# Two key copies from VectorE to ScalarE, and three issue costs in the list scheduler of an attention and feed-forward kernel

## The chip, the cores and the metric

The kernel runs on one core of one Trainium2 chip. The metric is the device time of one execution in microseconds (us), measured on that core. A kernel is executed six times where it is timed, in rounds that alternate with executions of the kernel before on the same chip. A "fast" run is one within 1.5% of the fastest of its kernel.

## The reference, cut to what matters

Attention with a threshold over 8 batches, 8 heads, 576 positions and 64 columns; then a row norm and a gated feed-forward layer over 4608 rows of 512.

```python
scores = (q @ k.transpose(0, 1, 3, 2)) / 8                    # 8 x 8 x 576 x 576
thresh = scores.max(-1, keepdims=True) - tau                  # tau = 0.02
scores = np.where(scores >= thresh, scores, -1e9)
attn = exp(scores - max); attn = attn / (attn.sum(-1) + 1e-9)
x = (attn @ v), heads laid side by side                       # 4608 x 512
xn = x / sqrt(mean(x * x) + 1e-6) * rms_g
out = (silu(xn @ w_gate) * (xn @ w_val)) @ w_out              # 512 -> 1536 -> 512
```

## The kernel before

The program is first written down as a list of operations, each with its engine, an assumed cost in ns, a priority, and the operations it needs. A list scheduler then fixes the order in which each engine's queue is filled. The costs in `COST` do nothing else: they are beliefs, and the chip never sees them.

```python
COST = dict(
    # ... cut: some 30 costs of PE, DVE, ACT and POOL operations ...
    sp=480.0, sp_v=650.0, sp_w=600.0, sp_tr=1300.0, sp_qk=900.0, sp_tl=630.0,     # DMA issues on SyncE
)
# ... cut ...
    seq = order_ops(ops, {"R": 4})        # always takes the operation that it believes can start first
    for o in seq:
        o.fn(o)                           # each call appends to its engine's queue, in this order
```

The work goes in 144 score steps, each a block of 128 query rows by a pair of heads. A step is: scores into PSUM (TensorE, L566); a row reduction per head (VectorE, L589), which also copies the scores out; the threshold from the row maxima (GpSimd, L596); masking and exponential (ScalarE L607 and L614, or with the mask on GpSimd, L626, L640 and L645); a transpose of the weights (on TensorE in early steps, L659, later by DMA); attention times values (L693, L697); the division (VectorE, L714 and L715). When a block has all its heads, its row norm (ScalarE L726, then GpSimd L729, L731, L734) and the feed-forward matmuls (gate L792, value L797, output L853) are dealt between later steps.

```python
    tn = add("POOL", COST["pool_tiny"], s - 4, [ttr_of[s, 0], ttr_of[s, 1]], nthr)     # threshold, L596
    # ...
    pls.append(add("ACT", COST["prelu"], s + 0.5, [tn], prelu))                        # masking pass, L607
    # ... in the row norm of a block:
    bb = add("POOL", COST["pool_mean"], s, [a, o_c], mean)                             # L729, L731
    c = add("POOL", COST["xn"], s - 1, [bb], norm)                                     # L734
```

At the start the keys of the four pairs of heads are transposed on TensorE (L364) and copied out of PSUM in halves, one half by each of two engines (L374):

```python
        def transposed(load, srcs, dsts, prio, engines):
            # ... transposes into one PSUM bank ...
            for e, (eng, lo, hi) in enumerate(engines):
                def ev(o, eng=eng, lo=lo, hi=hi):
                    copy = nc.scalar.copy if eng == "ACT" else nc.vector.tensor_copy
                    # ... copies parts lo to hi ...
        # ... in emit_k, for pair p:
            t, k_ready[p] = transposed(load, [pair(nat[:, 1, c]) for c in range(4)],
                                       [(0, 2, qkT[0][p][:, 1, 0:2]), (2, 2, qkT[0][p][:, 1, 2:4])], prio,
                                       [("DVE", 0, 2), ("ACT", 2, 4)])
```

## Time and profile before

| | kernel before |
|---|---|
| time, median of 3 runs ahead of the change | 567.91 us (567.86 to 568.21) |
| profiled span | 568.3 us |
| TensorE / ScalarE / VectorE / GpSimd busy | 98% / 80% / 75% / 57% |
| my estimate of pure TensorE work | 533 us |

The profiled span belongs to one execution, which took 570.23 us, slower than all six timed executions of the first comparison. So the span is good for finding where time goes, and the timed runs alone say how much it is. The busy table, the chain and the stages are read in the prediction. One more stretch turns out to matter. This is the timeline of the kernel before at 67 us, each line with its start, its duration, engine, line and operation, and in brackets the idle time ahead of it and what ended it:

```profile
67.32 1.28 POOL L645 TENSOR_TENSOR wsb<-wsb,esb 128x576 f16<-128x576 f16 x1
...
69.64 0.69 POOL L734 TENSOR_SCALAR xn<-xsb,ir 128x512 f16<-128x512 f32 x1
...
70.41 0.52 POOL L596 TENSOR_SCALAR nth<-mx 128x2 f32<-128x2 f32 x2
...
70.67 0.77 ACT L607 ACTIVATE ssb<-ssb,nth 128x576 f32<-128x576 f32 x1 [1.92 <-POOL nth L596]
```

GpSimd does a mask (L645), then the whole norm of a block (three instructions, of which the last is shown), and only then the thresholds of steps 19 and 20, the first a job of a quarter of a microsecond for which ScalarE has been idle for 1.92 us.

### The profile page before, as it was taken

What the parts mean: (1) busy time and instruction counts of PE and PEld (TensorE: products, weight loads), DVE (VectorE), ACT (ScalarE), POOL (GpSimd) and SP (SyncE); (2) the same over time, 40 slices, a digit from 0 to 9 for tenths busy, and PEclk for the clock granted to TensorE, in tenths of its full rate; (3) what the DMA queues carried; (4) which work ended last, traced back from release to release, by engine and by line L of the source; (5) the groups of instructions that cost most, each with busy time, mean ns of one, the idle gap of its engine ahead of it and who ended that gap; (6) DMA issues with size and microseconds to landing.
All of it is one profiled execution on the core that took longest, in us unless ns stands there. A gap on an engine that the chain in (4) does not pass through costs nothing.

```text
span 568.3 us, 13686 instructions
## 1 busy us (share of the span) xinstructions
PE 558.4 (98%) x5000; PEld 334.7 (59%) x5000; DVE 427.2 (75%) x1093; ACT 457.4 (80%) x739; POOL 322.4 (57%) x462
## 2 busy tenths in 40 slices
PE   8999999999999999999999999999999999999997
PEld 4666766767676555555555555545555455454674
DVE  4899977969958588758895789659875886586354
ACT  4999899999878787979898898778978897884332
POOL 2378946976747457666766658555666555551000
PEclk9999999999999999999999999999999999999999
DMA  8999998769994686999876799789887565633211
GB/s 187 250 289 282 178 195 184 161 132 202 167 202 104 136 159 149 177 177 187 178 160 148 142 186 181 161 168 162 174 167 184 88 96 86 178 81 44 84 37 38
DMA packets 270019, 88.98 MB, mean 157 GB/s; under 512 B 252544, under 2 KB 262272, under 8 KB 269952
## 3 DMA queue, kind: packets, MB, share of 16 engines
q1 hardware_dynamic: 267168, 86.02, 74.1%
q0 software_dynamic: 1600, 1.57, 1.8%
q8 instruction: 39, 0.64, 0.5%
q10 hardware_dynamic: 1184, 0.52, 0.3%
q14 instruction: 28, 0.23, 0.1%
HBM read 37.75 MB, written 9.44 MB: 83 GB/s over the span
## 4 chain that ended last, share of the span: by engine, by line
PE 89%; DVE 3%; DMA 2%; issue 2%; ACT 2%; POOL 1%; SPq 0%; DVEq 0%; POOLq 0%; ACTq 0%
PE s_ps L566 28%; PE ring L792 16%; PE ring L797 16%; PE ring L853 14%; PE ring L697 6%; PE ring L303 2%; PE ring L693 2%; DVE ssb L589 2%; DMA qkn<-in_q_dram 1%; PE s_ps L831 1%; PE s_ps L853 1%; PE ring L659 1%; PE s_ps L797 1%; PE ring L364 1%; DMA stage<-in_q_dram 1%
## 5 line engine op out<-in xcount | busy, mean ns | idle before, releaser
L589 DVE CUSTOM_DVE_ANT_0 ssb<-s_ps,zrow 128x576 f32<-128x576 f32 x288 | 207.8, 754 | 67.7 <-PE s_ps L566 60.5
L607 ACT ACTIVATE ssb<-ssb,nth 128x576 f32<-128x576 f32 x224 | 165.9, 766 | 32.4 <-POOL nth L596 32.1
L566 PE MATMUL s_ps<-qkt 64*128 64x288 f32 x1024 | 170.2, 429 | 1.4 <-DVE mx L589 1.1
L566 PEld LDWEIGHTS s_ps<-qkt 64*128 64x128 f32 x1024 | 96.2, 186 | 53.5 <-DVE mx L589 16.2
L640 POOL TENSOR_SCALAR wsb<-ssb,nth 128x576 f16<-128x576 f32 x64 | 110.5, 1726 | 9.7 <-DMA wt<-wsb 2.9
L792 PE MATMUL ring<-xnT,wg 128*128 128x512 f16 (+1 forms) x548 | 112.9, 328 | 0.4 <-DVE sl L809 0.4
L797 PE MATMUL ring<-xnT,wv 128*128 128x256 f16 (+1 forms) x544 | 111.4, 327 | 0.6 <-ACT qTv L472 0.3
L596 POOL TENSOR_SCALAR nth<-mx 128x2 f32<-128x2 f32 x144 | 31.6, 220 | 133.9 <-DVE mx L589 120.6
L809 DVE SCALAR_TENSOR_TENSOR sl<-th,ring 128x512 f32<-128x512 f32 (+1 forms) x137 | 75.9, 554 | 25.9 <-ACT th L806 24.6
L614 ACT ACTIVATE wsb<-ssb 128x1152 f16<-128x1152 f32 x80 | 92.9, 1161 | 1.9
L806 ACT ACTIVATE th<-ring 128x512 f32<-128x512 f32 (+1 forms) x137 | 66.3, 486 | 28.9 <-PE ring L792 26.4
L853 PE MATMUL ring<-wo,hf 128*128 128x512 f16 x384 | 89.3, 380 | 0.0
L645 POOL TENSOR_TENSOR wsb<-wsb,esb 128x576 f16<-128x576 f16 x64 | 81.8, 1278 | 8.8 <-ACT esb L626 4.4
L814 DVE TENSOR_TENSOR hf<-ring,sl 128x256 f16<-128x256 f32 (+1 forms) x136 | 75.9, 558 | 10.0 <-PE s_ps L566 0.5
L797 PEld LDWEIGHTS <-wv 128*128 128x128 f16 x576 | 52.2, 98 | 42.9 <-issue 12.3
L792 PEld LDWEIGHTS <-wg 128*128 128x128 f16 x576 | 52.0, 98 | 41.0 <-issue 11.6
L853 PEld LDWEIGHTS <-hf 128*128 128x128 f16 x408 | 37.4, 98 | 47.2 <-issue 6.6
L626 ACT ACTIVATE esb<-ssb,nth 128x576 f16<-128x576 f32 x64 | 49.2, 768 | 7.1 <-POOL nth L596 7.0
L697 PE MATMUL ring<-va,wt 128*128 128x65 f16 (+1 forms) x1264 | 52.8, 193 | 0.0
L697 PEld LDWEIGHTS <-wt 128*128 128x128 f16 (+1 forms) x1280 | 48.7, 100 | 3.4
L611 ACT ACTIVATE wsb<-ssb 128x576 f16<-128x576 f32 x64 | 43.6, 681 | 1.6
L693 PE MATMUL ring<-va,wt 128*128 128x130 f16 (+1 forms) x158 | 35.1, 227 | 0.1
(68 smaller groups left out, 448.1 us busy)
## 6 DMA issues: line engine op xcount, KB each, us to landing
vst<-in_v_dram SPq DMA_DIRECT2D x32, 256.0 KB, 3.2
qkn<-in_k_dram SPq DMA_DIRECT2D x31, 256.0 KB, 3.8
out_dram<-osb SPq DMA_DIRECT2D x31, 256.0 KB, 2.6
qkn<-in_q_dram SPq DMA_DIRECT2D x28, 256.0 KB, 4.1
stage<-in_moe_w_gate_dram SPq DMA_DIRECT2D x6, 512.0 KB, 6.6
stage<-in_moe_w_val_dram SPq DMA_DIRECT2D x6, 512.0 KB, 6.3
wt<-wsb SPq DMA_TRANSPOSE x128, 3.1
wo<-in_moe_w_out_dram POOLq DMA_DIRECT2D x4, 384.0 KB, 7.6
```

The source lines that it names most:

```text
L566: nc.tensor.matmul(s_ps[h][rows, ROW_AT + n * part:ROW_AT + n * part + n], lhs(hs), kT[i][p][h][hs, n * part:n * part + n], start=True, st ...
L589: nc.vector.tensor_tensor_reduce(out=ssb[a][:, h], in0=s_ps[h][:, ROW_AT:ROW_AT + S], in1=zrow, scale=-1.0 / 8.0, scalar=3.0e38, op0=ALU.a ...
L607: nc.scalar.activation(out=ssb[a][:, h], in_=ssb[a][:, h], func=PRELU, scale=-1.0, bias=nth[m][:, h:h + 1], **PRELU_KW)
L614: nc.scalar.activation(out=wsb[s % NW], in_=ssb[a], func=AF.Exp)
L640: nc.gpsimd.tensor_scalar(out=wsb[s % NW][:, h], in0=ssb[a][:, h], scalar1=nth[m][:, h:h + 1], scalar2=None, op0=ALU.is_le)
L645: nc.gpsimd.tensor_tensor(out=wsb[s % NW][:, h], in0=wsb[s % NW][:, h], in1=esb[es], op=ALU.mult)
L697: nc.tensor.matmul(ring[o.slot[0]][rs, at:at + D + 1], w[:, 5 * h + j, rs], va[vi][:, p, 2 * j + h], start=False, stop=(h == 1 and j == 3))
L792: nc.tensor.matmul(ring[o.slot[0]][:, 0:n], wg[d][:, fs], xnT[slot][:, d, 0:n], start=(d == 0), stop=(d == 3))
L797: nc.tensor.matmul(ring[o.slot[0]][:, 0:n], wv[d][:, fs], xnT[slot][:, d, 0:n], start=(d == 0), stop=(d == 3))
L809: nc.vector.scalar_tensor_tensor(out=sl[i][:, 0:n], in0=th[i][:, 0:n], scalar=1.0, in1=ring[g.slot[0]][:, 0:n], op0=ALU.add, op1=ALU.mult)
L814: nc.vector.tensor_tensor(out=hf[hi][:, 0:n], in0=ring[vv.slot[0]][:, 0:n], in1=sl[i][:, 0:n], op=ALU.mult)
L853: nc.tensor.matmul(ring[(first or o).slot[0]], hf[hs[fc][0]][:, 128 * j:128 * (j + 1)], wo[:, fc], start=(fc == 0), stop=(fc == NFC - 1))
```

## The change

The intent: take two copies off VectorE while it is the engine that holds up the first steps, and give the scheduler issue costs on SyncE nearer to those that the trace shows (a key or query load of one issue takes 0.61 to 0.65 us there from 21 to 52 us, but for one of 2.72; the constant was 0.90). No instruction is added or removed.

```diff
-    sp=480.0, sp_v=650.0, sp_w=600.0, sp_tr=1300.0, sp_qk=900.0, sp_tl=630.0,
+    sp=420.0, sp_v=600.0, sp_w=600.0, sp_tr=1300.0, sp_qk=680.0, sp_tl=630.0,
@@
-                                       [("DVE", 0, 2), ("ACT", 2, 4)])
+                                       [("ACT" if p in (1, 2) else "DVE", 0, 2), ("ACT", 2, 4)])
```

## The prediction

> **What bounds the kernel now.** I read the busy table first, then the chain of waits, then busy time by stage, then the first 17 us of the timeline. The page gives:
>
> ```profile
> PE 558.4 (98%) x5000; PEld 334.7 (59%) x5000; DVE 427.2 (75%) x1093; ACT 457.4 (80%) x739; POOL 322.4 (57%) x462
> ...
> PE 89%; DVE 3%; DMA 2%; issue 2%; ACT 2%; POOL 1%; SPq 0%; DVEq 0%; POOLq 0%; ACTq 0%
> ```
>
> TensorE is busy 98% and is 89% of the chain that ends last; no other engine is over 80%. A busy TensorE may still be a waiting one (the spans of its matmuls are modelled), so I also counted its work: the instructions of the built program, times the spacing that the chain shows when they run back to back. 128 ordinary score steps at 1.17 us and 16 of the 64-row kind at 1.14 are 168 us. Gate and value matmuls, 2 x (288 x 0.216 + 288 x 0.109), are 187; output matmuls, 432 x 0.216, 93; attention times values, 1280 x 0.031 + 160 x 0.06, 49; transposes of queries and keys, 28 x 0.64, 18; of weights, 16 x 0.61, 10; the rest about 8. My estimate is 533 us of pure TensorE work. Of the other 35 us, 6.3 lie before the first score operands are there and 4.0 after the last matmul, so **some 25 us are holes** in the middle, and no reordering can be worth more.
>
> Where are they? I laid the start of each step's first row reduction against the TensorE work queued before that step. The lag grows from 5.4 us at step 0 to 18.5 us at step 36 (122.9 us into the span), and only by 12 us more over the last 108 steps. So half of the holes are in the first fifth of the run. Busy time by stage (PE, PEld, DVE, ACT, POOL, then clock, DMA share, GB/s) shows why:
>
> ```profile
> 0.00:10.00 10.00, 8.62 (x37) 4.66 (x37) 3.92 (x16) 3.35 (x9) 0.69 (x6) 1.00 0.79 174
> 10.00:20.00 10.00, 9.45 (x63) 5.86 (x63) 7.86 (x22) 8.82 (x13) 4.14 (x10) 1.00 0.98 225
> 20.00:30.00 10.00, 9.03 (x127) 7.16 (x126) 9.05 (x26) 9.39 (x15) 3.90 (x8) 1.00 1.06 279
> 30.00:40.00 10.00, 8.94 (x116) 6.79 (x115) 8.95 (x25) 9.17 (x13) 7.99 (x17) 1.00 1.14 283
> ...
> 500.00:510.00 10.00, 10.00 (x70) 4.96 (x67) 9.09 (x20) 8.87 (x15) 6.39 (x7) 1.00 0.40 89
> ```
>
> From 10 to 60 us ScalarE and VectorE are both near 9 of 10 and the DMA engines are full: this stage goes at the pace of the softmax. Each step needs two masking passes of 0.72 and one exponential of 1.16 on ScalarE, 2.6 us, plus its share of copies and squares; steps 8 to 12 indeed start 2.9 us apart. Later TensorE is without visible gaps.
>
> **What the Trainium skill says.** "Perfetto Trace Analysis", section Optimization Strategy, says that a kernel may have several regimes with different most-contended engines, to be dealt with each for itself; the table above agrees (ScalarE 9.39 of 10 at 20 to 30 us, TensorE later). The same page, section Optimizing Scalar/DVE Operations, has the fixed cost of an access to PSUM lower on ScalarE (about 51 ns) than on VectorE (about 125), and advises moving work to ScalarE where VectorE is saturated. The trace agrees on the size: the 128x256 copy out of PSUM takes 0.42 us on VectorE and 0.36 on ScalarE. "PSUM — Partial Sum Buffer", section PSUM bank collisions raise a hardware error, says that two engines must not touch one bank and quadrant at once, so the copies of two engines out of one bank must run in turn. The trace shows that turn: ScalarE is held 5.0 us in all, 3 times, by a VectorE copy of the same keys. "DMA: Bandwidth & Descriptors", section Issuing engines are not separate DMA queues, says that all issues share the same 16 engines; an issue moved ahead on one queue therefore moves others back.
>
> **The change part by part.**
>
> *The copies.* For pairs 1 and 2 (the second and third) the first half of the keys is copied by ScalarE instead of VectorE. VectorE loses 2 x 0.42 = 0.84 us, ScalarE gains 2 x 0.36 = 0.72. The timeline of before:
>
> ```profile
> 8.42 0.76 DVE L589 CUSTOM_DVE_ANT_0 ssb<-s_ps,zrow 128x576 f32<-128x576 f32 x1 [0.87 <-PE s_ps L566]
> ...
> 9.02 0.96 ACT L374 COPY qkt<-ring 128x256 f32<-128x256 f32 x3 [1.00 <-PE ring L364]
> ...
> 9.43 0.42 DVE L374 COPY qkt<-ring 128x256 f32<-128x256 f32 x1 [0.24 <-ACT qkt L374]
> ...
> 9.77 0.75 DVE L589 CUSTOM_DVE_ANT_0 ssb<-s_ps,zrow 128x576 f32<-128x576 f32 x1
> ```
>
> VectorE waits 0.24 for ScalarE's half, copies for 0.42, and only then starts the second reduction at 9.77; without the copy it can start at 9.18, so 0.6 us earlier. But the second step's scores need ScalarE's copies, five by then: 9.02 + 2 x 0.36 + 2 x 0.30 = 10.3, against 9.90 before. Its second half waited till 10.64 for the reduction, so that step ends some 0.3 us sooner at best. ScalarE, the tightest engine from there on, does two more copies (to 11.0) and starts its first masking pass at about 11.0 against 11.16. Afterwards its 1.44 + 1.16 + 0.35 bring it to 13.95, where the second step's passes began before (13.96). On the path that sets the end the part is worth **0.1 us, at most 0.4**.
>
> *The ordering's costs.* Three constants (480 to 420, 650 to 600, 900 to 680) are only beliefs of the list scheduler about what an issue takes on SyncE. No instruction is added or removed by them: TensorE has 7493 rows in both, SyncE 336. But every queue is re-dealt; the two programs differ on 13,890 lines of TensorE. Read in the new order: the first load of batch 1's keys goes before a value load instead of after; transposes of batch 1's pair 0 move behind step 6 and of pair 1 before step 7 (they were behind it). That load's queries were issued at 22.04 and took 6.0 us, to 28.04; TensorE would get to them at about 27.2, so a wait of up to 0.8 us is possible there, given back one step later, where a transpose is gone. By step 18 the new queue has 1.3 us more gate/value work ahead of the score step, which falls in the stage with holes; by step 26 the two are level. From step 78 to 100 it has 3.5 to 5.8 us more ahead, and 2.6 us more ahead of the last score step; TensorE is saturated there, so that trades places and moves no end. I estimate **1 us gained** out of the 13 us of early holes, by choice rather than by a view: better issue times should on balance make a better order.
>
> Sum: 567.9 - 0.1 - 1.1 = **566.7 us**.
>
> **The rivals.** (a) *Nothing at all*: the pure work is the same, ScalarE bounds the early stage and gets 0.7 us more to do. For it: ScalarE idles just 3.4 us between 10 and 50 us. It would give 567.6 to 568.2. (b) *A worse deal*: in-order queues block on a load or a bank that the scheduler thought ready, as at the pair 1 transposes, or the DMA queue, at full share already, brings batch 1 or the weights later. Against it: only one TensorE wait on a load is on record before (0.8 us). It would give 569 to 571. (c) *A better deal*: the holes of the first 130 us shrink by a quarter, since the lag there is not forced by any single engine. It would give 564 to 565. (d) *TensorE itself changes*: a lower granted clock, for instance; before it was 0.999 and nothing in the change touches it.
>
> **Range and chances.** The certain part is a tenth of a microsecond; all else is the re-dealing of some 13 us of early holes, and I take a fifth of that, about 3 us, to either side of the middle: **563.7 to 569.5**. 2% is 11.4 us, nearly all of the early holes at once for faster, and doubling them for slower. **Faster 0.015, same 0.97, slower 0.015.**
>
> **What would show it.** Right: VectorE's second reduction at about 9.2 instead of 9.77; the first masking pass on ScalarE at 11.0 within 0.2; TensorE's lag at step 0 to 6 within 0.5 us of before; total TensorE work unchanged, and the whole difference already there when the first 130 us are over. Wrong: a new TensorE wait on a load of over 1 us; a lag that differs in the last 400 us, where I take TensorE for saturated; a longer tail after the last matmul than 4.0 us; or a start, before step 0, that isn't the same in both.

## The result, and the profile after

The changed kernel takes **566.56 us** (median of six, 565.68 to 568.14) against 567.88 (566.68 to 568.94) for the kernel before in the same rounds: a ratio of 0.9982, with a 95% interval from 0.9962 to 1.0003. Outputs are correct. A ratio here is always the mean time of one kernel's fast runs over that of the other's of the same rounds, so it isn't quite the ratio of the medians quoted beside it.

The span of the profile after is 563.6 us, 4.7 below before, but that execution was the fastest of its six (565.68 us) and the one before was slow (570.23). The traces differ by more than the kernels do; this has to be kept in mind in all that follows.

The busy table and the chain after:

```profile
PE 555.8 (99%) x5000; PEld 333.7 (59%) x5000; DVE 425.8 (76%) x1091; ACT 460.3 (82%) x741; POOL 322.4 (57%) x462
...
PE 94%; DMA 2%; DVE 1%; issue 1%; POOL 1%; ACT 1%; SPq 0%; DVEq 0%; POOLq 0%
```

Two instructions have gone from VectorE to ScalarE, as the diff says, and TensorE's share of the chain rose from 89 to 94%: fewer steps of the chain are waits. The start of the changed kernel, to be held against the timeline in the prediction:

```profile
8.93 1.85 ACT L374 COPY qkt<-ring 128x256 f32<-128x256 f32 x6 [1.12 <-PE ring L364]
...
9.01 0.75 DVE L589 CUSTOM_DVE_ANT_0 ssb<-s_ps,zrow 128x576 f32<-128x576 f32 x1
...
10.66 1.45 ACT L607 ACTIVATE ssb<-ssb,nth 128x576 f32<-128x576 f32 x2
...
11.69 0.75 DVE L589 CUSTOM_DVE_ANT_0 ssb<-s_ps,zrow 128x576 f32<-128x576 f32 x1
...
12.37 0.42 DVE L374 COPY qkt<-ring 128x256 f32<-128x256 f32 x1
```

The second reduction starts at 9.01 (before 9.77) and ScalarE's six copies run back to back in 1.85 us. The last two lines are the second reduction of step 1, right behind the first (at 11.00), and the copy for the fourth pair, which follows both. In the kernel before that copy stood between the two:

```profile
11.46 0.76 DVE L589 CUSTOM_DVE_ANT_0 ssb<-s_ps,zrow 128x576 f32<-128x576 f32 x1 [0.60 <-PE s_ps L566]
...
12.50 0.42 DVE L374 COPY qkt<-ring 128x256 f32<-128x256 f32 x1 [0.27 <-PE ring L364]
...
12.84 0.75 DVE L589 CUSTOM_DVE_ANT_0 ssb<-s_ps,zrow 128x576 f32<-128x576 f32 x1
```

And the stretch of step 19's threshold, after:

```profile
66.10 0.22 POOL L596 TENSOR_SCALAR nth<-mx 128x2 f32<-128x2 f32 x1
...
66.66 0.19 POOL L729 TENSOR_SCALAR irm<-ssq 128x1 f32<-128x1 f32 x1 [0.34 <-ACT xn L726]
...
67.05 0.76 ACT L607 ACTIVATE ssb<-ssb,nth 128x576 f32<-128x576 f32 x1
```

The new order deals the threshold ahead of the norm, and the masking pass on ScalarE (the last line) has no idle time listed ahead of it any more.

**A lag for each step.** To find where the lead arises I used the measure of the prediction: the start of a step's first reduction, less the TensorE work queued ahead of that step (each instruction of the order at its back-to-back duration, 535.4 us in all; the rounded terms of the prediction gave 533). Where this lag grows there is a hole in TensorE's work. As the order itself differs between kernels, plain start times can't be compared; lags can, best between points where both orders have about the same work behind them (at step 72 229.7 and 230.5 us, at the end the same). Growth of the lag in us, by steps, in one traced execution of each:

| kernel | 0→2 | 20→22 | 22→36 | lag at 36 | lag at 72 | 72→end |
|---|---|---|---|---|---|---|
| before | 1.64 | 1.99 | 1.53 | 18.5 | 24.6 | 8.3 |
| changed | 0.58 | −0.04 | 2.54 | 16.1 | 20.9 | 7.3 |

At the end the lags are 32.9 and 28.2, which is the 4.7 us between the spans: 2.4 of it is there by step 36 (119 us into the span of the changed kernel), 1.3 more by step 72, and 1.0 comes after that, where I had taken TensorE for saturated. The new order has two early holes less (at steps 0 to 2 and 20 to 22), but pays about half of the second one back by step 36.

### The profile page after: what moved, and what is told of

Same layout as the page of the kernel before. It is cut to its first block, busy times and chain, and to the rows that moved or that the text cites. A ratio compares the mean times of both kernels' runs of the same rounds, so it can differ in the third digit from the quotient of the medians.

```text
span 563.6 us, 13681 instructions
## 1 busy us (share of the span) xinstructions
PE 555.8 (99%) x5000; PEld 333.7 (59%) x5000; DVE 425.8 (76%) x1091; ACT 460.3 (82%) x741; POOL 322.4 (57%) x462
## 3 DMA queue, kind: packets, MB, share of 16 engines
q0 software_dynamic: 1600, 1.57, 1.8%
## 4 chain that ended last, share of the span: by engine, by line
PE 94%; DMA 2%; DVE 1%; issue 1%; POOL 1%; ACT 1%; SPq 0%; DVEq 0%; POOLq 0%
PE s_ps L566 29%; PE ring L792 16%; PE ring L797 16%; PE ring L853 15%; PE ring L697 6%; PE ring L303 2%; PE ring L693 2%; PE ring L659 1%; PE ring L364 1%; DMA qkn<-in_q_dram 1%; PE s_ps L797 1%; PE s_ps L831 1%; PE s_ps L853 1%; PE s_ps L261 1%; DVE ssb L589 1%
## 5 line engine op out<-in xcount | busy, mean ns | idle before, releaser
L566 PE MATMUL s_ps<-qkt 64*128 64x288 f32 x1024 | 168.4, 430 | 0.4 <-DVE mx L589 0.4
L792 PE MATMUL ring<-xnT,wg 128*128 128x256 f16 (+1 forms) x564 | 114.4, 325 | 0.3 <-DVE xsb L715 0.3
L797 PE MATMUL ring<-xnT,wv 128*128 128x512 f16 (+1 forms) x528 | 110.4, 332 | 0.0
L809 DVE SCALAR_TENSOR_TENSOR sl<-th,ring 128x256 f32<-128x256 f32 (+1 forms) x141 | 77.1, 547 | 30.4 <-ACT th L806 29.8
L806 ACT ACTIVATE th<-ring 128x256 f32<-128x256 f32 (+1 forms) x141 | 67.7, 480 | 33.2 <-PE ring L792 28.7
L814 DVE TENSOR_TENSOR hf<-ring,sl 128x512 f16<-128x512 f32 (+1 forms) x132 | 75.0, 568 | 9.3 <-PE ring L797 0.5
```

Of the source, the lines that this page charges most:

```text
L566: nc.tensor.matmul(s_ps[h][rows, ROW_AT + n * part:ROW_AT + n * part + n], lhs(hs), kT[i][p][h][hs, n * part:n * part + n], start=True, st ...
L792: nc.tensor.matmul(ring[o.slot[0]][:, 0:n], wg[d][:, fs], xnT[slot][:, d, 0:n], start=(d == 0), stop=(d == 3))
L797: nc.tensor.matmul(ring[o.slot[0]][:, 0:n], wv[d][:, fs], xnT[slot][:, d, 0:n], start=(d == 0), stop=(d == 3))
L809: nc.vector.scalar_tensor_tensor(out=sl[i][:, 0:n], in0=th[i][:, 0:n], scalar=1.0, in1=ring[g.slot[0]][:, 0:n], op0=ALU.add, op1=ALU.mult)
L814: nc.vector.tensor_tensor(out=hf[hi][:, 0:n], in0=ring[vv.slot[0]][:, 0:n], in1=sl[i][:, 0:n], op=ALU.mult)
```

## The experiments

Three theories at the outset. **R** (re-dealing): the gain comes from the new order; the copies add next to nothing. **C** (copies): the gain is the two copies off VectorE. **N** (nothing): 0.2% is noise. Three places within R were then tested singly, the threshold at step 19, the copy between the reductions, and the score steps late in the run, and last the reason for which the new order should be better at all.

### The same program again

The kernel before with a comment at its end.

> The kernel before, unchanged but for a comment: the null. All theories expect a ratio of 1.000 within its interval. What it measures is how far two identical programs come apart: if its median is 1 us or more from that of before, or single runs span over 2 us, then the 1.3 us between the two kernels is of the size of the noise, and the 4.7 us between the two traces (568.3 and 563.6) is mostly a slow and a fast execution.

Measured: 568.98 us (567.84 to 570.96) against 569.17 (566.73 to 571.18), ratio 1.0009 [0.9985, 1.0033]. This is the size of the noise: one program spreads over 4.5 us on one chip, and six runs give its ratio to within 0.24%, or 1.4 us. Its trace shows where the spread arises: from step 53 to 143 its lag grows as that of the kernel before, to 0.02 us (7.44 and 7.42), while from step 2 to 20 it grew by 8.86 us instead of 7.88. The two executions part in the first fifth of the run, where the DMA engines are at full share.

### The copies alone, in the old order

```diff
-                                       [("DVE", 0, 2), ("ACT", 2, 4)])
+                                       [("DVE", 0, 2), ("ACT", 2, 4)], ["ACT" if p in (1, 2) else "DVE", "ACT"])
```

The added list names the engines that the copies run on; the scheduler still sees the old ones. All other queues are as before.

> The two key copies on ScalarE, all queues otherwise in the order of before (TensorE, GpSimd and SyncE are identical to before). Theory A (my prediction: the copies are worth 0.1 to 0.4 us, the rest is the new order): first masking pass at 10.7 to 11.1 us instead of 11.16, end 0.1 to 0.5 us earlier, ratio 0.9992 to 1.000. Theory B (the copies are the whole gain, as the second step's reductions come 1.1 us earlier): ratio about 0.998, 1.0 to 1.3 us. Theory C (all is noise): ratio 1.000 and no shift in the first 20 us of the trace either.

Measured: 568.42 us (567.38 to 569.6), 0.9993 [0.997, 1.0017]. In its trace the lag grows by 1.40 us from step 0 to 2, against 1.64 before: the copies give 0.24 us, and the clock doesn't see it. The first masking pass came at 10.50 us, earlier than the 10.7 to 11.1 expected, but the first reduction of this execution had already started 0.34 us early. The interval still holds the whole gain of the change, so C isn't out yet; the next run decides.

### The new order, the copies on VectorE

The mirror image: costs and copies as in the change for the scheduler, but the two copies run on VectorE.

```diff
-    sp=480.0, sp_v=650.0, sp_w=600.0, sp_tr=1300.0, sp_qk=900.0, sp_tl=630.0,
+    sp=420.0, sp_v=600.0, sp_w=600.0, sp_tr=1300.0, sp_qk=680.0, sp_tl=630.0,
@@
-                                       [("DVE", 0, 2), ("ACT", 2, 4)])
+                                       [("ACT" if p in (1, 2) else "DVE", 0, 2), ("ACT", 2, 4)], ["DVE", "ACT"])
```

> The order of the changed kernel, with the two copies back on VectorE where before had them. Theory A: it keeps most of the gain, 0.8 to 1.2 us, ratio 0.998 to 0.9987. Theory B: it is back at the time of before, ratio 1.000. If the order is even harmful without the copies: over 1.000.

Measured: 566.75 us (566.21 to 567.45), 0.9966 [0.9946, 0.9986]. The order alone gives the gain, and the interval leaves 1 out. (The gain is larger than theory A expected, but the interval reaches into A's range.) Its lag grows 0.89 from step 0 to 2, so most of the early lead belongs to the order too. C falls as the main cause, R stands.

### The changed kernel again

Only a comment added, on the chip of the three above.

> The changed kernel again on the same chip as the two halves of it. All but the noise theory expect the ratio of the first measurement, 0.998 (0.9962 to 1.0003), now with a narrower joint interval; theory A expects it to be the product of the two halves within 0.001. The noise theory expects 0.9995 to 1.0005.

Measured: 567.13 us (565.93 to 568.62), 0.9974 [0.9952, 0.9997]. The interval leaves out 1, if only just, so N is unlikely. Theory A expected the product of the two halves within 0.001; that is 0.9959, so this missed by 0.0015 in all, which is within the noise of the three ratios. A wait that I had not foreseen shows best in this execution. TensorE's waits from 18 to 80 us, and its line at 23 us:

```profile
PE ring L364 <- DMA qkn<-in_q_dram: 1.8, 1, 1.8
...
23.36 0.52 PE L364 MATMUL ring<-id,qkn 128*128 128x128 f32 x3 [1.82 <-DMA qkn<-in_q_dram]
```

In the first execution of the same program it was a third of that:

```profile
22.49 0.52 PE L364 MATMUL ring<-id,qkn 128*128 128x128 f32 x3 [0.60 <-DMA qkn<-in_q_dram]
```

Here TensorE waits for the queries of the fourth pair. The new order issues them behind a load of gate weights (the two lines are of SyncE's queue in the changed kernel):

```profile
16.01 0.47 SPq L916 DMA_DIRECT2D stage<-in_moe_w_gate_dram  x1
...
16.58 0.94 SPq L354 DMA_DIRECT2D qkn<-in_q_dram  x2
```

This execution is 0.4 us ahead of the other one of the same program at step 2 and 1.9 us behind it at step 18, and stays behind by 1.9 to 2.2 us to the end. So the change also brought a wait that the old order doesn't have at this place. What it costs in the end is tested further below.

### The threshold ahead of the norm, in the old order

One swap: on GpSimd the norm of one block goes behind the threshold of step 19. The helper serves the next experiments too; it takes an operation out of the finished order and puts it right behind another.

```diff
     seq = order_ops(ops, {"R": 4})
+    def behind(what, other):
+        seq.remove(what)
+        seq.insert(seq.index(other) + 1, what)
+    for o in norm_op[3]:
+        behind(o, nth_op[19])
```

> The order of before with one swap on GpSimd: the threshold of step 19 ahead of the row normalisation of the fourth block, instead of behind it (no other row of any queue moves). Theory A (this swap, which the new order also has, is the largest single part of the gain): ScalarE's idle of 1.9 us before its masking pass at 70.67 us is gone, the growth of TensorE's lag at step 21 falls from +1.65 to under +0.3, and nothing gives it back: the end comes 1.2 to 1.7 us earlier, ratio 0.997 to 0.998. Rival B (the idle is slack; ScalarE or TensorE waits again within the next ten steps): the step 21 hole goes, but the lag at step 28 and the time are as before, ratio 0.9995 to 1.0005.

The swap did in the trace what it should:

```profile
68.61 0.22 POOL L596 TENSOR_SCALAR nth<-mx 128x2 f32<-128x2 f32 x1
68.91 0.19 POOL L729 TENSOR_SCALAR irm<-ssq 128x1 f32<-128x1 f32 x1
...
69.34 0.77 ACT L607 ACTIVATE ssb<-ssb,nth 128x576 f32<-128x576 f32 x1
```

The threshold comes at 68.61, right behind the mask, ScalarE's masking pass has no wait listed any more, and the lag grows by 0.44 us from step 20 to 22, instead of 1.99 to 2.02 in the traces of the kernel before, of the same again and of the copies alone. (Two later traces that keep this part of the old order have 1.31 and 1.44, so the hole itself scatters.) From step 22 to 36 it gives nothing back (1.53 as before). Yet timed it is 566.86 us (566.39 to 568.21) against 567.22, 0.999 [0.9971, 1.0009]. The hole is real and the change closes it; what it is worth at the end is between 1.6 us gained and 0.5 lost, and the middle (0.6) is less than the 0.9 to 1.6 us that the traces show at the place. Its size isn't settled.

### The fourth pair's copy behind both reductions, in the old order

```diff
+    behind(k_copy[3][0], ttr_of[1, 1])
```

> The order of before with one swap on VectorE: the first half of pair 3's keys is copied behind the second row reduction of step 1, not ahead of it. Theory A: the lag at step 2 grows by 0.6 us instead of 1.3 since step 0, as in every run of the new order, but as ScalarE sets the pace of the next 15 steps, at most 0.3 us of it is left by step 18: ratio 0.9990 to 1.0003. Rival B (an early gain is carried to the end): 0.7 us, ratio 0.9987.

Its lag grows 0.93 us from step 0 to 2, not 1.64: this one swap makes the 0.7 us of early lead that are not the copies'. Timed: 567.6 us (567.14 to 570.72), 1.0009 [0.9985, 1.0033]. Nothing of it is seen at the end, though 0.9 us lies within the interval. A lead at step 2 has to pass through the stage of full DMA engines, where executions of one program already part by more.

### One of the three costs alone

```diff
-    sp=480.0, sp_v=650.0, sp_w=600.0, sp_tr=1300.0, sp_qk=900.0, sp_tl=630.0,
+    sp=480.0, sp_v=650.0, sp_w=600.0, sp_tr=1300.0, sp_qk=680.0, sp_tl=630.0,
```

> Of the change just one constant: 680 instead of 900 for an issue of a pair's queries or keys; the copies and the two other constants as before. Its queues show both swaps of the last two runs and the new order of loads up to the batch 1 pairs. Theory A (those early swaps are what the new order is worth): 1.0 to 2.0 us faster, ratio 0.9965 to 0.9985, lag growth at step 21 under +0.3. Rival (the gain hangs on the whole of the new order): ratio 0.999 to 1.001.

Measured: 566.72 us (566.05 to 567.53), 0.9984 [0.9966, 1.0002]: the same as the whole change within the noise. As the interval holds 1, this run alone doesn't part theory A from its rival. Its order is a third one: the lag grows 0.93 from step 0 to 2 and 0.38 from 20 to 22, but 3.24 from 22 to 36, so that from 20 to 36 it loses as much as the old order (3.6 and 3.5 us). From step 72 to the end it loses 7.3 us as the changed kernel does. What it has in common with the changed kernel is thus not all at the hole of step 20: it is also TensorE's queue late in the run, as the next run makes plain.

### The costs moved the other way

The change's copies, but each of the three constants moved up by about as much as the change moves it down, away from what the trace shows.

```diff
-    sp=480.0, sp_v=650.0, sp_w=600.0, sp_tr=1300.0, sp_qk=900.0, sp_tl=630.0,
+    sp=540.0, sp_v=700.0, sp_w=600.0, sp_tr=1300.0, sp_qk=1120.0, sp_tl=630.0,
@@
-                                       [("DVE", 0, 2), ("ACT", 2, 4)])
+                                       [("ACT" if p in (1, 2) else "DVE", 0, 2), ("ACT", 2, 4)])
```

> The changed kernel with the three constants moved away from the trace by as much as the change moved them towards it: 540, 700 and 1120 instead of 480, 650 and 900. Theory A (a new order helps where it happens to mend a swap, whatever the constants): this order has the threshold of step 19 ahead of the normalisation too, so no hole at step 21; between 0.5 and 2.0 us faster than before, ratio 0.9965 to 0.999. Rival (truer issue times make a better order): slower than before, ratio 1.001 or more.

Measured: 566.21 us (565.41 to 566.84), 0.9971 [0.9952, 0.9991]. This is the most telling run. Wrong costs are as good as true ones. The lag grows by 1.60 from step 0 to 2 as in the old order, but by −0.02 from 20 to 22 and by 7.3 from 72 to the end as in the new one. So **it isn't the truth of the costs that made the order better**.

But these are not three independent deals. Laid side by side, TensorE's queues of the changed kernel, of one cost alone and of the costs the other way are the same from step 73 on, but for one exchange at step 116. The traces show it: of the last 2500 weight loads on TensorE, 15 stand at another place in each of these two than in the changed kernel, against 1657 in the kernel before. So all re-dealt kernels try one late order only.

### Score steps moved apart, in the old order

From step 72 to the end the old order loses about 1 us more than the new ones. In its chain of waits (start, duration, what) some score steps are stretched, two of them to 1.57 us, while most take 1.17:

```profile
265.79 1.57 PE s_ps L566 x8
...
285.50 1.57 PE s_ps L566 x8
...
333.98 1.30 PE s_ps L566 x8
...
404.16 1.30 PE s_ps L566 x8
```

The two long ones stand where there is little other work since the last score step (1.2 us). The chain of the changed kernel has one stretched step from step 72 on:

```profile
402.83 1.31 PE s_ps L566 x8
```

So the old order has some 0.9 us more of stretch in its chain. Theory: the stretch is the loss. Two swaps on TensorE lengthen these intervals.

```diff
+    last_behind_score(75, "gmm")     # the gate group ahead of score step 75 goes behind it
+    score_behind_next(82, "vmm")     # the value group behind score step 82 goes ahead of it
```

> The order of before with two moves on TensorE alone: one gate group from ahead of score step 75 to behind it, one value group from behind step 82 to ahead of it, so that the two intervals of 2.46 us of work between score steps 75 and 76 and between 81 and 82 hold 3.3. Theory A (a score step that comes too soon after the last one waits inside its own matmuls for the second row reduction: 1.57 us in place of 1.17, also where TensorE looks saturated): the pieces of 1.57 at 265.8 and 285.5 us in the chain become 1.17, the lag grows 0.7 to 0.9 us less between steps 72 and 96, end 0.6 to 0.9 us earlier, ratio 0.9984 to 0.999. Rival B (TensorE is saturated there; moving work changes nothing): lag growth 2.74 as in all runs of the old order, ratio 1.000.

The chain of this kernel at the two places:

```profile
262.49 1.32 PE s_ps L566 x8
...
285.93 0.43 DVE xsb L715
286.36 0.04 issue
286.40 1.02 PE ring L797 x4
```

The two pieces of 1.57 are gone, but the lag grows by 3.5 us from step 72 to 96, more than the 2.7 of the old order, and the time is 568.96 us (567.09 to 570.79) against 568.6, 1.002 [0.9998, 1.0043]. The loss of 0.8 us at the place is about the loss on the clock (0.2%, 1.1 us). The first swap only moved the stretch to the step before; the second made the value group wait for VectorE's division (the line of L715 in the chain) to free its PSUM bank. These two swaps gain nothing. The theory isn't settled by them, since each put another wait in place of the stretch that it took away: the 0.9 us by which the chains differ in stretched steps would be most of the 1.0, but no run took the stretch away alone. What makes the 1.0 us less from step 72 on is located, and its cause stays open.

### Both swaps of the old order together

```diff
+    for o in norm_op[3]:
+        behind(o, nth_op[19])
+    last_behind_score(75, "gmm")
+    score_behind_next(82, "vmm")
```

> Both mends in the order of before: the threshold of step 19 ahead of the normalisation and the two moved groups; no constant and no copy changed. Theory A (the gain of the change is such places in the order, and they add up): 1.5 less at steps 20 to 22 and 0.8 less at 72 to 96, 1.5 to 2.3 us faster than before, ratio 0.996 to 0.9975, level with the changed kernel within 0.7 us. Rival B (only the whole new order does it): ratio over 0.9985.

Measured: 568.45 us (567.91 to 569.2) against 568.6, 1.0011 [0.9994, 1.0029]. Theory A (0.996 to 0.9975) is out: the two swaps together are no part of the gain on the clock. The product of the two single ratios is 0.999 × 1.002 = 1.001, so the parts add, as far as noise of 0.2% lets one say. The lag grows by 0.45 from step 20 to 22 and by 3.5 from 72 to 96, as in the two kernels apart: in the trace the effects don't touch each other.

### The new order, the query load first

Mends the wait that the change brought: the first gate weights are issued behind the fourth pair's queries.

```diff
+    behind(w_load[0], q_load[3])     # on top of the changed kernel
```

> The changed kernel with one swap on SyncE: the last three quarters of pair 3's queries are loaded ahead of the first gate weights, not behind. Theory A: TensorE's wait for them near 22 us (0.6 and 1.8 us in two traces of the changed kernel) is under 0.3, and as it is the largest part of the spread between executions, the median falls by 0.3 to 1.0 us against the changed kernel on the same chip and the runs lie closer. Rival B (the softmax catches up or a weight comes late): the wait goes, the time is that of the changed kernel within 0.3 us.

No wait on that load is listed any more. Measured: 566.24 us (566.03 to 567.43), 0.9974 [0.9954, 0.9993], 0.3 us below the changed kernel's own 566.57 in the same rounds: within noise. In its trace part of what it has by step 22 is given back: the lag grows 3.45 us from step 22 to 36, against 2.54 in three traces of the changed kernel. Its six runs span 1.4 us instead of 2.5, which would fit the lost wait, but six runs are few for that. Of the 0.3 to 1.0 us expected, no more than the rival's 0.3 is seen.

### The changed kernel, a third time

> The changed kernel on this chip, to be set beside the last three runs. Both theories: ratio 0.9965 to 0.9985. It is there for the comparison, not to tell the theories apart.

Measured: 566.57 us (565.74 to 568.28), 0.9981 [0.9959, 1.0003]. Three of its runs lie at 565.7 to 565.8 and three at 567.3 to 568.3.

**All runs side by side** (ratios to the kernel before of the same rounds):

| old order | ratio | re-dealt order | ratio |
|---|---|---|---|
| the same again | 1.0009 | changed, three comparisons | 0.9982, 0.9974, 0.9981 |
| copies alone | 0.9993 | copies back on VectorE | 0.9966 |
| threshold ahead of norm | 0.9990 | one cost alone | 0.9984 |
| fourth pair's copy behind | 1.0009 | costs the other way | 0.9971 |
| even scores | 1.0020 | query load first | 0.9974 |
| threshold and even scores | 1.0011 | | |

Every kernel with the old order, mended by hand or not, is at 0.9990 or above; every one with a re-dealt order is at 0.9984 or below. No version beats the changed kernel beyond the noise. The traces part them in the same way:

| traced execution | 0→2 | 20→22 | lag at 72 | 72→end |
|---|---|---|---|---|
| old: before; the same again | 1.64; 1.63 | 1.99; 2.02 | 24.6; 25.3 | 8.3; 8.4 |
| old: copies alone | 1.40 | 2.00 | 23.5 | 8.4 |
| old: threshold ahead of norm | 1.62 | 0.44 | 22.2 | 8.3 |
| old: fourth pair's copy behind | 0.93 | 1.44 | 21.4 | 8.4 |
| old: even scores; with the threshold | 1.81; 1.77 | 1.31; 0.45 | 24.5; 22.3 | 9.1; 9.1 |
| new: changed, three traces | 0.58 to 0.89 | −0.04 | 20.9 to 23.1 | 7.3 to 7.4 |
| new: copies back on VectorE | 0.89 | −0.03 | 21.5 | 7.5 |
| new: one cost alone | 0.93 | 0.38 | 22.0 | 7.3 |
| new: costs the other way | 1.60 | −0.02 | 22.0 | 7.3 |
| new: query load first | 0.57 | −0.03 | 22.0 | 7.3 |

The last column parts old from new most cleanly, and within an order it hardly scatters. That is less evidence than its many rows suggest: from step 73 on all old rows but the two with even scores have one TensorE queue, and all new rows have another, so this is a comparison of two orders, measured often. It gives 1.0 us, which would be most of the 1.2 us that the clock shows. That it is what the clock shows is argued from the traces; no run put the late order alone into the old kernel. (The second column parts them too, if barely: 0.44 against 0.38.) The lag at step 72 scatters by 2.2 us between traces of the changed kernel alone, so what the early holes give can't be read from single traces.

## Why the prediction was right or wrong

The total is right: 566.7 us predicted, 566.56 measured, and three comparisons give a mean ratio of 0.9979, or 1.2 us gained where the sum had 0.1 + 1.1 (the text of the prediction estimates 1 us for the order, its sum takes 1.1). That it came so close is luck: the 1 us was put down by choice, for a reason that fell, and the first comparison alone allows for anything from 2.2 us gained to 0.2 lost. By its steps:

- **The copies, 0.1 and at most 0.4 us: not contradicted.** 0.24 in the trace of the copies alone; the clock, at 0.9993 ± 0.0024, can't tell this from nothing. In the new order two traces with the copies and the one without grow alike from step 0 to 2 (0.89). The second reduction was put at 9.2 and came at 9.01.
- **ScalarE's copies: a size was off.** The first masking pass was to start at 11.0 within 0.2 us and started at 10.66. The sum had four 128x256 copies at 0.36 us and two small ones (64x192) at 0.30, 2.04 us in all; from the first copy to the start of the masking pass it was 1.73, since in a row the instruction behind a 128x256 copy started 0.26 to 0.27 us after it, and not 0.36. The second step's scores came at 9.73 and not at 10.3 for another reason: the first of them started 0.16 us after the second copy had ended, so they didn't wait for the "five by then". The first masking pass was thus half a microsecond ahead of before rather than 0.16.
- **The new order, 1 us: the size about right, the reason wrong.** I wrote that better issue times should on balance make a better order. The costs moved the wrong way gave 0.9971. What holds is weaker: the old order was a poor draw beside the others that were tried. It has a threshold behind a norm, a copy between two reductions and about 1 us more loss in the second half of the run; the one other late order that was tried, which all re-dealt kernels share, lacks the last of these.
- **Where the gain lies: wrong.** The whole difference was to be there at 130 us. By step 36 it was 2.4 of 4.7 us in the two traces, and the early part is the one that scatters; 1.0 us arises after step 72, in every trace of the re-dealt kernels. The step that failed is "TensorE is saturated there, so that trades places and moves no end". From step 72 to the end the lag grows by 8.3 us in the old order and 7.3 in the new ones: a TensorE without visible gaps still had an eighth of these 8.3 us to give.
- **Waits: half right.** The wait at the second pair's transposes of batch 1 (up to 0.8 us) didn't come; a wait on another load did, 0.6 us in one execution and 1.8 in another, for queries that had been dealt behind the gate weights. I had read that loads change places, but only followed batch 1's.
- **Work, clock and ends: right.** The same work on TensorE, a clock of 1.0, the lag at step 0 within 0.1 us of before (5.33 and 5.42), and 4.05 us after the last matmul (4.04 before).
- **The lag at steps 0 to 6 within 0.5 us of before: wrong.** From step 2 to 6 it was 0.9 to 1.2 us lower. The prediction had not seen the fourth pair's copy between the two reductions of step 1, which the new order deals behind both.
- **A reading of a wait: too large.** Of the 5.0 us for which ScalarE was said to be held by VectorE's copies, 3.4 are one wait that ended at 6.16 us; VectorE's copy had itself begun only at 5.70, so at most 0.5 of it is the turn of the two engines.

Rival (a), nothing at all, would have been hard to tell from the truth by one comparison (0.9982 with 1 inside the interval); it took the order without the copies, and the change run again, to set it aside. Rival (b) happened in one place, the load; rival (c) happened too, but with its 1.2 us at a third of what it supposed and, by the traces, in good part late in the run. Three things stay open: what each early hole is worth at the end, since both swaps that closed one stayed within noise; which difference in the late order makes the 1.0 us; and whether it is this that the clock shows.

## What to carry to other kernels

Where a scheduler fixes in-order queues, a change to its costs is a new draw from orders that differ by some tenths of a per cent, whatever the truth of the costs: judge it by trying several draws, also wrong ones, before crediting the reason, and lay the drawn queues side by side: three draws here were one and the same order in the second half of the run. Look for short jobs that stand behind long ones on a half-idle engine (the threshold behind the norm), since no busy share shows them, and close such a hole by one swap before believing its size. And hold two traces of one program against each other first: here they differed by more than the kernels did.

## What the Trainium skill lacked or had wrong

- "Perfetto Trace Analysis", section Optimizing Scalar/DVE Operations, says that of the profiled latency of an access to memory one half, the write acknowledgement, overlaps with the next instruction. There is an overlap: in the changed kernel 128x256 copies out of PSUM on ScalarE took 0.37 us each, but the instruction behind one started 0.26 to 0.27 us after it. A sum over copies must take the second figure, and the section has no worked example of that.
- "DMA: Bandwidth & Descriptors", section Latency and other measured facts, gives the access to HBM as 0.2 us on average and 2 at high load. It has nothing on how long a load waits when the engines are at full share: queries issued at 16.58 us let TensorE go on at 22.49 in one execution of the changed kernel, and in another, issued at 16.70, at 23.36.
- No page has the scatter between executions of one program: 566.7 to 571.2 us in eleven runs of the kernel before on one chip, and a lag of 13.1 us at step 18 in one trace of the changed kernel against 15.0 in another.
- No page names the order of a queue as the reason why an engine that is far from full holds up another: GpSimd, 57% busy, held ScalarE for 1.92 us with a short operation behind long ones.
